# Statistics in one block, fitted planning costs, and an accumulating DMA inside the cross product

## The chip, the cores and the metric

The kernel runs on one core of one Trainium2 chip. Times are device microseconds of one execution; the time of a kernel is the median of its runs. A profile comes from one execution, whose own time is given beside its span. The engines are called as the profile calls them: PE (matrix multiplications, with its weight loads as PEld), DVE (vector), ACT (scalar and activation), POOL (GpSimd) and SP, which here only issues DMAs.

## The reference: what is computed

With q = x, k, v of 2048 x 640 (sequence by channel):

```python
g = sigmoid((x * gate_w).sum(-1, keepdims=True))
# a: causal 4-tap shift of k, times v, then a long convolution along the sequence, times q
kv = k_shift * v
y  = irfft(rfft(pad(kv)) * rfft(pad(ssm_k)))[:S] + kv * ssm_D
a  = q * y
# b: an MLP over the sequence axis
h  = layernorm(x)                       # over the 640 channels
u  = gelu(einsum("bsd,sf->bdf", h, w1) + b1)      # f = 1536
b  = transpose(einsum("bdf,fs->bds", u, w2) + b2)
out = g * a + (1 - g) * b
```

All inputs and the output are bf16.

## The kernel before

The long convolution is done in the frequency domain by matrix products with sine and cosine tables (`FTB`, and its transposed copy `GTB`, written by four DMA transposes). The sequence index is split as 4 residues (p = 0 to 3) by 128 partitions by 4 blocks (hk = 0 to 3); the two halves of the sequence (h = 0, 1) are transformed separately. `fwd` multiplies tables with one half of the weights (`wT`, name W) or of kv (name A); ACT evicts each result from PSUM into one of the arrays `C[0]` to `C[3]`; `mixing` combines the four residues by sums and differences on DVE. W gives the spectra V0 and V1, kv gives A0 and A1. `v1mix` adds one part of the weights' spectra onto another with accumulating DMAs on POOL's queue.

The products of spectra run on DVE in bf16. A spectrum holds slabs of 2560 columns: 1280 columns of one component and 1280 of the other. `cross(g)` (g = 0, 1; i = 0, 1 in each) multiplies A0 by V1 and leaves the result in V1; `y1(g)` forms A1 times V0 in A1 with `product` and adds V1 to it by `acc_dma`, an accumulating DMA on POOL's queue. `product(A0[g], ...)` gives the spectrum of the first half of the output. `invmix` turns spectra into four slabs `Z`, `inverse(h, Z)` multiplies by `GTB`, ACT evicts with the gate as scale into `cgb`, DVE multiplies by q (`q_hi`, `q_lo`) and adds onto the MLP's part in `O1`, and SP writes the rows out. `tm[0]` and `tm[1]` are the DVE's two scratch arrays for products.

Beside it stands the MLP. `ln_tile` takes statistics of one of 16 tiles of X on DVE, `ln_apply` computes the factors on POOL (a power) and normalizes X in place on DVE. Twelve groups of 32 matmuls (name m1, X by the columns of w1 in `ring`) are evicted with Gelu into `GT`; 16 groups of 24 (name m2, `GT` by w2 in `W2`, which takes over the space of `ring`) are evicted by ACT into `O1`. The gate's sums come from DVE products into three buffers `gq` and ACT copies with an accumulator (`gsum`), between the m1 groups.

PSUM has four slots, at most three for the convolution and two for the MLP. **The order on each engine is not that of the program text.** `SC.add` records every operation with a duration estimated by a formula (`dve_dur`, `act_dur`, `mms`, literal numbers for a few), its reads and writes and a priority: the place in the text, or a given number; the lower goes first, and the MLP's matmuls have the highest numbers. `SC.run` then plays a list schedule of all engines from these estimates: each engine takes the ready operation of lowest number. `SC.emit` writes the instructions in that order, with semaphore waits where an operation depends on another engine or a DMA. On the chip every engine executes its list in order, and a late operand holds up all that stands behind it in the list. An element-wise operation of n columns on POOL is charged n/500 + 0.3 us, a DMA of n bytes n/320000 us one after the other and 2.0 us more to its end.

Most helpers issue through a common line: L617 is any `tensor_tensor`, L627 and L628 any `tensor_scalar`, L655 any ACT operation, L293 any matmul, L262 an accumulating DMA, L260 a DMA transpose, L267 any other DMA.

Buffers overlap in place: before, `gq` and `junk` (the output of the gate's ACT copies) lie over `KF`, the taps' array of the k shift; `q_hi` lies over `C[0]`; `q_lo` over the second half of `C[1]`; one of the two arrays `kp`, through which k is transposed, lies over `GTB`.

Of the kernel before, what the change touches and what calls it, by code (L numbers as in the profile page):

```python
# [322 lines left out]
class _Sched:  # L323
# [58 lines left out]
    def run(self):  # L382
# [29 lines left out]
        while started < n:  # L412
# [6 lines left out]
            for e in engs:  # L419
                while pend[e] and pend[e][0][0] <= t:  # L420
                    _, p, i = heapq.heappop(pend[e])
                    heapq.heappush(ready[e], (p, i))
                if free[e] > t:
                    nxt.append(free[e])
                    continue
                skipped = []
                pick = None
                while ready[e]:
                    p, i = heapq.heappop(ready[e])
                    op = ops[i]  # L430
                    if op.vt is not None and op.vt.slot is None:
                        c = op.vt.cls
                        if not nfree or held.get(c, 0) >= self.limit.get(c, 99):
                            skipped.append((p, i))
                            continue
                    pick = op
                    break
                for s in skipped:
                    heapq.heappush(ready[e], s)
                if pick is None:  # L440
                    if pend[e]:
                        nxt.append(pend[e][0][0])
                    continue
                op = pick
                progress = True
                started += 1
                if op.vt is not None and op.vt.slot is None:
                    nfree.sort()
                    op.vt.slot = nfree.pop(0)
                    held[op.vt.cls] = held.get(op.vt.cls, 0) + 1  # L450
                op.start = t
                if e in ("SP", "QA") or op.lat < 0:
                    issue = 0.1
                    s = max(t + issue, dma_free)
                    dma_free = s + op.dur
                    op.end = dma_free + 2.0
                    free[e] = t + issue
                else:
                    op.end = t + op.dur
                    free[e] = op.end  # L460
                order.append(op)
                if op.vt is not None:
                    op.vt.left -= 1
                    if op.vt.left == 0:
                        heapq.heappush(frees, (op.end + 0.05, op.vt.slot, op.vt.cls))
                for s in op.asucc:
# [12 lines left out]
                nxt.append(free[e])  # L479
# [25 lines left out]
def _build(nc, A_q, A_k, A_v, A_shift_k, A_ssm_k, A_ssm_D, B_x, B_w1, B_b1, B_w2, B_b2, gate_w, out):  # L505
# [10 lines left out]
    with ExitStack() as es:  # L516
# [33 lines left out]

        gwb = alloc("gwb", [128, D], BF16)
        Drow = alloc("Drow", [1, D], BF16)
        ident = alloc("ident", [128, 128], BF16)
        KF = alloc("KF", [128, NG, 7, 32], BF16)
# [5 lines left out]
        rstd = alloc("rstd", [128, 16], F32)  # L560
        vtmp = alloc("vtmp", [128, 16], F32)
        gpre = alloc("gpre", [128, 16], F32)
# [157 lines left out]
        def k_turn(hk):  # L720
            o, i = kp[hk % 2], kn[hk % 2]
            ov = o[:, :, :].rearrange("p g (q c) -> p g q c", q=4)
            iv = V(i, 0, [[32, NG], [D, 4], [1, 32]])
            SC.add("DVE", 0.85, lambda s: T.op("DVE", lambda e: e.tensor_copy(ov, iv), [i[:, :, :]], [o[:, :, :]]), [i[:, :, :]], [o[:, :, :]], prio=0, name="kperm")  # L724
            c0 = 16 + 128 * (hk % 2)
# [114 lines left out]
        def ln_tile(hk, p):  # L840
            t = 4 * hk + p
            xs = X[:, hk, p, :]
            for ci in range(2):
                o, i = stats[:, t, 6 * ci:6 * ci + 6], xs[:, 320 * ci:320 * ci + 320]
                SC.add("DVE", 0.46, (lambda o, i: lambda s: T.op("DVE", lambda e: e.bn_stats(o, i), [i], [o]))(o, i), [i], [o])  # L845
            o, i = mv[:, t, :], stats[:, t, :]
            SC.add("DVE", 0.2, (lambda o, i: lambda s: T.op("DVE", lambda e: e.bn_aggr(o, i), [i], [o]))(o, i), [i], [o])
# [84 lines left out]
        for ft in range(FT):  # L932
# [14 lines left out]
            if ft == 0:  # L947
                act(junk[:, :], gwb[:, :], ACT.Copy, acc=gws[:, :], name="gws").after.add(g_)
# [17 lines left out]

        def w2_load(hk):
            for a in range(2):
                dma(W2[hk % 2][:, 6 * a:6 * a + 6, :], dr(B_w2, a * 6 * 128 * S + 512 * hk, [[S, 128], [128 * S, 6], [1, 512]]), 128 * 6144)

        for p in range(4):
            dma(GTB[:, p, :, :, :, :].rearrange("q a b c d -> q (a b c) d"), FTB[:, p, :, :, :, :].rearrange("q a b c d -> q (a b c) d"), 128 * 2048, rate=200.0, transpose=True, prio=10 ** 5)

        HORD = (2, 3, 0, 1)
        for n_, hk in enumerate(HORD):
            w2_load_at = n_
            W2h = W2[n_ % 2]
            for a in range(2):
                dma(W2h[:, 6 * a:6 * a + 6, :], dr(B_w2, a * 6 * 128 * S + 512 * hk, [[S, 128], [128 * S, 6], [1, 512]]), 128 * 6144)
            for p in range(4):  # L980
# [172 lines left out]
```

## Time and profile before

| | |
|---|---|
| median of 3 runs | 198.19 us (197.91 to 199.74) |
| profiled execution | 197.93 us, its span 196.1 us |
| PE busy | 177.4 us (90%) |
| DVE busy | 177.0 us (90%) |
| ACT busy | 118.5 us (60%) |
| POOL busy | 28.6 us (15%) |
| granted PE clock | 0.996 of full |
| HBM read, written | 25.87 MB, 2.62 MB |

A line of the timeline reads: start, length, engine, program line, operation, output<-input by the program's names without buffer numbers, shapes, count, and in brackets the idle time of that engine just before and who released it. Consecutive instructions of one kind are merged into one line with a count. "Issue to landing" of a DMA is the time from its issue to its completion.

### The profile page before, as it was taken

What the parts mean: (1) busy time and instruction counts of PE and PEld (TensorE: products, weight loads), DVE (VectorE), ACT (ScalarE), POOL (GpSimd) and SP (SyncE); (2) the same over time, 40 slices, a digit from 0 to 9 for tenths busy, and PEclk for the clock granted to TensorE, in tenths of its full rate; (3) what the DMA queues carried; (4) which work ended last, traced back from release to release, by engine and by line L of the source; (5) the groups of instructions that cost most, each with busy time, mean ns of one, the idle gap of its engine ahead of it and who ended that gap; (6) DMA issues with size and microseconds to landing.
All of it is one profiled execution on the core that took longest, in us unless ns stands there. A gap on an engine that the chain in (4) does not pass through costs nothing.

```text
span 196.1 us, 3370 instructions
## 1 busy us (share of the span) xinstructions
PE 177.4 (90%) x1403; PEld 131.4 (67%) x1403; DVE 177.0 (90%) x196; ACT 118.5 (60%) x187; POOL 28.6 (15%) x30
## 2 busy tenths in 40 slices
PE   0759987999999999999999999999999979997890
PEld 0546564468767787777777778888888867775560
DVE  7996998799999179999999879999999599989994
ACT  4798967997749793799796413131313117664471
POOL 2629802500005400000000000040400000000000
PEclk9999999999999999999999999999999999999998
DMA  5999999994999999960053008029999960222034
GB/s 162 331 409 379 364 209 253 310 417 143 165 276 265 227 199 191 258 202 0 3 185 135 3 24 282 15 64 232 234 305 231 383 269 5 91 76 101 3 107 160
DMA packets 36719, 37.62 MB, mean 192 GB/s; under 512 B 15579, under 2 KB 32608, under 8 KB 36704
## 3 DMA queue, kind: packets, MB, share of 16 engines
q1 hardware_dynamic: 34464, 32.15, 54.4%
q0 software_dynamic: 2176, 5.24, 14.4%
q8 instruction: 11, 0.18, 0.4%
q14 instruction: 4, 0.03, 0.0%
q10 hardware_dynamic: 64, 0.01, 0.0%
HBM read 25.87 MB, written 2.62 MB: 145 GB/s over the span
## 4 chain that ended last, share of the span: by engine, by line
PE 67%; DVE 16%; DMA 9%; ACT 3%; POOL 2%; issue 2%; SPq 0%; DVEq 0%
PE pp L293 67%; DMA kn<-in_A_k_dram 5%; DMA X<-in_A_q_dram 4%; DVE kp L724 3%; DVE stats L845 2%; DVE C L617 2%; DVE SS L617 2%; DVE X L628 2%; ACT ksh L655 2%; DVE vkv L617 1%; DVE cgb L617 1%; DVE O L617 1%; POOL rstd L617 1%; POOL vtmp L627 1%; ACT cgb L655 1%
## 5 line engine op out<-in xcount | busy, mean ns | idle before, releaser
L293 PE MATMUL pp<-X,ring 128*128 128x320 bf16 x384 | 55.5, 299 | 1.6 <-DVE X L628 1.6
L617 DVE TENSOR_TENSOR C<-C 128x2560 bf16<-128x2560 bf16 (+1 forms) x28 | 48.9, 1773 | 8.3 <-ACT C L655 5.5
L293 PE MATMUL pp<-GT,W 128*128 128x320 bf16 x384 | 52.8, 299 | 1.1 <-ACT O L655 1.1
L293 PEld LDWEIGHTS pp<-GT,W 128*128 128x128 bf16 x384 | 43.5, 113 | 10.0 <-issue 1.4
L293 PEld LDWEIGHTS pp<-X,ring 128*128 128x128 bf16 x384 | 36.6, 98 | 17.6 <-DVE X L628 2.0
L655 ACT ACTIVATE C<-pp 128x640 bf16<-128x640 f32 x64 | 39.9, 723 | 5.5 <-PE pp L293 5.2
L655 ACT ACTIVATE O<-pp,c,omg 128x640 bf16<-128x640 f32 (+1 forms) x17 | 14.5, 853 | 37.9 <-PE pp L293 37.9
L617 DVE TENSOR_TENSOR tm<-C,C 128x2560 bf16<-128x2560 bf16 (+1 forms) x12 | 22.8, 1930 | 0.0
L262 POOL DMA_DIRECT2D C<-C x6 | 7.5, 1406 | 90.1 <-DVE C L617 90.1
L293 PE MATMUL pp<-wT,FTB 128*128 128x320 bf16 x128 | 20.2, 314 | 0.4 <-ACT wT L655 0.4
L655 ACT ACTIVATE GT<-pp,cc 128x640 bf16<-128x640 f32 x12 | 9.5, 792 | 14.6 <-PE pp L293 14.5
L617 DVE TENSOR_TENSOR C<-tm 128x1280 bf16<-128x1280 bf16 (+1 forms) x16 | 18.0, 1154 | 0.1
L293 PEld LDWEIGHTS pp<-wT,FTB 128*128 128x128 bf16 x128 | 11.9, 102 | 7.8 <-ACT C L655 2.3
L655 ACT ACTIVATE cgb<-pp,gg 128x640 bf16<-128x640 f32 x16 | 12.6, 794 | 6.4 <-PE pp L293 3.3
L293 PE MATMUL pp<-C,GTB 128*128 128x320 bf16 x96 | 13.7, 299 | 2.2 <-DVE C L617 2.2
L293 PE MATMUL pp<-ident,ssm 128*128 128x128 bf16 x80 | 8.4, 265 | 6.2 <-DVE pint L617 5.3
L845 DVE BATCH_NORM_STATS2 stats<-X 128x6 f32<-128x320 bf16 x32 | 13.5, 460 | 0.4 <-DMA X<-in_A_q_dram 0.4
L293 PEld LDWEIGHTS pp<-C,GTB 128*128 128x128 bf16 x96 | 9.2, 98 | 6.4 <-DVE C L617 2.5
L655 ACT ACTIVATE junk<-gq 128x640 bf16<-128x640 bf16 x16 | 11.8, 737 | 0.5
L293 PEld LDWEIGHTS pp<-ident,ssm 128*128 128x128 bf16 x80 | 6.5, 127 | 8.0 <-DMA ssm<-in_A_ssm_k_dram 5.3
L655 ACT ACTIVATE wT<-pp 128x640 bf16<-128x640 f32 x16 | 10.2, 711 | 2.6 <-PE pp L293 2.6
L655 ACT ACTIVATE ksh<-pp 128x1024 bf16<-128x1024 f32 (+1 forms) x12 | 9.6, 893 | 3.2 <-PE pp L293 3.2
(63 smaller groups left out, 176.6 us busy)
## 6 DMA issues: line engine op xcount, KB each, us to landing
ring<-in_B_w_dram SPq DMA_DIRECT2D x12, 512.0 KB, 10.9
W<-in_B_w_dram SPq DMA_DIRECT2D x8, 768.0 KB, 6.9
C<-C POOLq DMA_DIRECT2D x6, 640.0 KB, 11.3
ssm<-in_A_ssm_k_dram SPq DMA_DIRECT2D x4, 640.0 KB, 9.0
X<-in_A_q_dram SPq DMA_DIRECT2D x4, 640.0 KB, 9.3
kn<-in_A_k_dram SPq DMA_DIRECT2D x4, 640.0 KB, 8.5
out_dram<-O SPq DMA_DIRECT2D x7, 320.0 KB, 2.3
vkv<-in_A_v_dram SPq DMA_DIRECT2D x2, 640.0 KB, 4.7
```

Source lines behind the costliest of these rows:

```text
L262: ins = engobj.dma_start(out_ap, in_ap, accum_op=ALU.add, max_dma_last_dim=2560)
L293: ins = self.nc.tensor.matmul(ps_ap, lhsT=lhsT, rhs=rhs, start=start, stop=stop, skip_group_check=True)
L617: return SC.add(eng, d, lambda s: T.op(eng, lambda e: e.tensor_tensor(o, a, b, op), [a, b], [o]), [a, b], [o], prio=prio, name="tt")
L627: return e.tensor_scalar(o, a, s1, None, op0=op0)
L628: return e.tensor_scalar(o, a, s1, s2, op0=op0, op1=op1)
L655: return T.op("ACT", lambda e: e.activation(o, src, func, **kw), rr + [src], ww)
L724: SC.add("DVE", 0.85, lambda s: T.op("DVE", lambda e: e.tensor_copy(ov, iv), [i[:, :, :]], [o[:, :, :]]), [i[:, :, :]], [o[:, :, :]], prio ...
L845: SC.add("DVE", 0.46, (lambda o, i: lambda s: T.op("DVE", lambda e: e.bn_stats(o, i), [i], [o]))(o, i), [i], [o])
```

## The change

Six things are changed together:

- **Planning costs.** The constants of `dve_dur`, `act_dur`, `mms`, `kperm`, `bn_stats` and `bn_aggr` are different, and DMAs on POOL's queue are charged 3 us more to their end. These numbers enter no instruction; they enter the order.
- **Statistics.** `ln_apply` is called once after all 16 tiles, on 16 columns, in place of four calls on 4 columns; one more POOL product keeps sqrt(var) in `sd`, which replaces one small DVE product of the gate.
- **Cross product.** The first multiplication of 2560 columns is made into two of 1280 (one into `V1` in place, one into a quarter of `tm[0]`), and their sum is formed by a DMA that accumulates `tm[0]`'s quarter onto `V1`. The other sum stays on DVE, with the two halves of `tm[1]` used in turn.
- **Space of q_hi and gq.** `q_hi` moves over `Drow` and `KF`, and is loaded ahead of the W2 loads in the text; `gq` moves from `KF` over `GTB`; `junk` goes, the ACT copies write in place.
- **q_lo** is loaded only after the last W2 load has been issued.
- **product(A0[0])** stands behind `inverse(1, Z1)` in the text instead of ahead of its `invmix`.

```diff
@@ SC.run
-                    op.end = dma_free + 2.0
+                    op.end = dma_free + 2.0 + (3.0 if e == "POOL" else 0.0)
@@ buffers
+        ident = alloc("ident", [128, 128], BF16)
         Drow = alloc("Drow", [1, D], BF16)
-        ident = alloc("ident", [128, 128], BF16)
...
-        gq = [alloc(f"gq{i}", [128, 2, D], BF16, at=base_of(KF) + 2560 * i) for i in range(3)]
-        junk = alloc("junk", [128, D], BF16, at=base_of(KF) + 7680)
+        gq = [alloc(f"gq{i}", [128, 2, D], BF16, at=base_of(GTB) + 2560 * i) for i in range(3)]
...
-        q_hi = alloc("q_hi", [128, 2, 4, D], BF16, at=base_of(C[0]))
+        q_hi = alloc("q_hi", [128, 2, 4, D], BF16, at=base_of(Drow))
@@ planning costs
-            return n / {1: 960.0, 2: 1920.0, 4: 3840.0}[mode] + (0.1 if mode == 4 else 0.16)
+            return n / {1: 960.0, 2: 1920.0, 4: 3840.0}[mode] + (0.04 if mode == 4 else 0.08)
-            return n / 1200.0 + 0.19 + 0.09 * nap
+            return n / 1200.0 + 0.09 + 0.05 * nap
-            dur = sum(max(n_of(r) / 2400.0, 0.06) for _, _, r, _, _ in items)
+            dur = sum(max(n_of(r) / 2400.0 + 0.0025, 0.056) for _, _, r, _, _ in items)
...
@@ statistics
-        def ln_apply(hk):
-            r = slice(4 * hk, 4 * hk + 4)
-            ts("POOL", vtmp[:, r], mv[:, r, 1], 1e-5, None, ALU.add)
-            tt("POOL", rstd[:, r], vtmp[:, r], V(cst, 1, [[0, 4]]), ALU.pow)
-            for p in range(4):
-                t = 4 * hk + p
-                ts("DVE", X[:, hk, p, :], X[:, hk, p, :], mv[:, t, 0:1], rstd[:, t:t + 1], ALU.subtract, ALU.mult, mode=4, extra=0.17)
+        def ln_apply():
+            ts("POOL", sd[:, :], mv[:, :, 1], 1e-5, None, ALU.add)
+            tt("POOL", rstd[:, :], sd[:, :], V(cst, 1, [[0, 16]]), ALU.pow)
+            tt("POOL", sd[:, :], sd[:, :], rstd[:, :], ALU.mult)
+            for t in range(16):
+                xs = X[:, t // 4, t % 4, :]
+                ts("DVE", xs, xs, mv[:, t, 0:1], rstd[:, t:t + 1], ALU.subtract, ALU.mult, mode=4, extra=0.16)
...
-                    ln_apply(hk)
+                ln_apply()
@@ gate
-                        act(junk[:, :], gb[:, b, :], ACT.Copy, acc=gacc[:, t:t + 1], name="gsum")
-        tt("DVE", gth[:, :], vtmp[:, :], rstd[:, :], ALU.mult, mode=1, prio=0)
-        tt("DVE", gth[:, :], gth[:, :], gacc[:, :], ALU.mult, mode=1, prio=0)
+                        act(gb[:, b, :], gb[:, b, :], ACT.Copy, acc=gacc[:, t:t + 1], name="gsum")
+        tt("DVE", gth[:, :], sd[:, :], gacc[:, :], ALU.mult, mode=1, prio=0)
@@ q_hi (ahead of the W2 loads)
+        for kt in range(2):
+            dma(q_hi[:, kt, :, :], dr(A_q, (1024 + 512 * kt) * D, [[4 * D, 128], [1, 4 * D]]), 128 * 5120)
@@ cross
+        ncr = [0]
         def cross(g):
             for i in range(2):
-                tt("DVE", half(T1, 0), half(A0[g], i), half(V1[g], i), ALU.mult)
-                tt("DVE", half(T1, 1), half(A0[g], i), half(V1[g], i, True), ALU.mult)
-                tt("DVE", comp(V1[g], i, 0), comp(T1, 0, 0), comp(T1, 0, 1), ALU.add)
-                tt("DVE", comp(V1[g], i, 1), comp(T1, 1, 1), comp(T1, 1, 0), ALU.subtract)
+                n_ = ncr[0]
+                ncr[0] += 1
+                tmp = V(tm[0], 1280 * (n_ % 4), [[1, 1280]])
+                tt("DVE", half(T1, n_ % 2), half(A0[g], i), half(V1[g], i, True), ALU.mult)
+                tt("DVE", tmp, comp(A0[g], i, 1), comp(V1[g], i, 1), ALU.mult)
+                tt("DVE", comp(V1[g], i, 0), comp(A0[g], i, 0), comp(V1[g], i, 0), ALU.mult)
+                tt("DVE", comp(V1[g], i, 1), comp(T1, n_ % 2, 1), comp(T1, n_ % 2, 0), ALU.subtract)
+                dma(comp(V1[g], i, 0), tmp, 128 * 5120, stream="POOL", prio=0, accum=True)
@@ the end
-        for kt in range(2):
-            dma(q_hi[:, kt, :, :], dr(A_q, (1024 + 512 * kt) * D, [[4 * D, 128], [1, 4 * D]]), 128 * 5120)
-        product(A0[0], A0[0], V0[0])
         Z1 = invmix(A1[0], A1[1], C3a, None, None)
         inverse(1, Z1)
...
-            dma(q_lo[:, kt, :, :], dr(A_q, 512 * kt * D, [[4 * D, 128], [1, 4 * D]]), 128 * 5120)
+            dma(q_lo[:, kt, :, :], dr(A_q, 512 * kt * D, [[4 * D, 128], [1, 4 * D]]), 128 * 5120).after.add(w2last)
+        product(A0[0], A0[0], V0[0])
         product(A0[1], A0[1], V0[1])
```

More of the change, by code (lines that the diff above doesn't have):

```diff
@@ L560, in _build @@
         rstd = alloc("rstd", [128, 16], F32)
-        vtmp = alloc("vtmp", [128, 16], F32)
+        sd = alloc("sd", [128, 16], F32)
         gpre = alloc("gpre", [128, 16], F32)
@@ L598, in _build @@
         q_lo = alloc("q_lo", [128, 2, 4, D], BF16, at=base_of(C[1]) + 2 * SL * 2)
-        q_hi = alloc("q_hi", [128, 2, 4, D], BF16, at=base_of(C[0]))
+        q_hi = alloc("q_hi", [128, 2, 4, D], BF16, at=base_of(Drow))
+        assert base_of(KF) == base_of(Drow) + 1280
         cgb = [alloc(f"cgb{i}", [128, 2, D], BF16, at=base_of(FTB) + 2560 * i) for i in range(3)]
@@ L723, in k_turn @@
             iv = V(i, 0, [[32, NG], [D, 4], [1, 32]])
-            SC.add("DVE", 0.85, lambda s: T.op("DVE", lambda e: e.tensor_copy(ov, iv), [i[:, :, :]], [o[:, :, :]]), [i[:, :, :]], [o[:, :, :]], prio=0, name="kperm")
+            SC.add("DVE", 0.75, lambda s: T.op("DVE", lambda e: e.tensor_copy(ov, iv), [i[:, :, :]], [o[:, :, :]]), [i[:, :, :]], [o[:, :, :]], prio=0, name="kperm")
             c0 = 16 + 128 * (hk % 2)
@@ L844, in ln_tile @@
                 o, i = stats[:, t, 6 * ci:6 * ci + 6], xs[:, 320 * ci:320 * ci + 320]
-                SC.add("DVE", 0.46, (lambda o, i: lambda s: T.op("DVE", lambda e: e.bn_stats(o, i), [i], [o]))(o, i), [i], [o])
+                SC.add("DVE", 0.38, (lambda o, i: lambda s: T.op("DVE", lambda e: e.bn_stats(o, i), [i], [o]))(o, i), [i], [o])
             o, i = mv[:, t, :], stats[:, t, :]
-            SC.add("DVE", 0.2, (lambda o, i: lambda s: T.op("DVE", lambda e: e.bn_aggr(o, i), [i], [o]))(o, i), [i], [o])
-        def ln_apply(hk):
-            r = slice(4 * hk, 4 * hk + 4)
-            ts("POOL", vtmp[:, r], mv[:, r, 1], 1e-5, None, ALU.add)
-            tt("POOL", rstd[:, r], vtmp[:, r], V(cst, 1, [[0, 4]]), ALU.pow)
-            for p in range(4):
-                t = 4 * hk + p
-                ts("DVE", X[:, hk, p, :], X[:, hk, p, :], mv[:, t, 0:1], rstd[:, t:t + 1], ALU.subtract, ALU.mult, mode=4, extra=0.17)
+            SC.add("DVE", 0.12, (lambda o, i: lambda s: T.op("DVE", lambda e: e.bn_aggr(o, i), [i], [o]))(o, i), [i], [o])
+        def ln_apply():
[5 more added lines that the diff above has]
+                ts("DVE", xs, xs, mv[:, t, 0:1], rstd[:, t:t + 1], ALU.subtract, ALU.mult, mode=4, extra=0.16)
         srcW = lambda h: (lambda kt, p, ci: wT[:, 2 * h + kt, p, 320 * ci:320 * ci + 320])
@@ L947, in _build @@
             if ft == 0:
-                act(junk[:, :], gwb[:, :], ACT.Copy, acc=gws[:, :], name="gws").after.add(g_)
+                act(gq[2][:, 0, :], gwb[:, :], ACT.Copy, acc=gws[:, :], name="gws").after.add(g_)
             if ft in (1, 3, 5, 7):
@@ L965, in _build @@
         tt("DVE", c2[:, :].rearrange("p (a b) -> p a b", a=4), omg[:, :].rearrange("p (a b) -> p a b", a=4), b2f, ALU.mult, mode=1, prio=0)
-        def w2_load(hk):
-            for a in range(2):
-                dma(W2[hk % 2][:, 6 * a:6 * a + 6, :], dr(B_w2, a * 6 * 128 * S + 512 * hk, [[S, 128], [128 * S, 6], [1, 512]]), 128 * 6144)
         for p in range(4):
@@ L974, in _build @@
         HORD = (2, 3, 0, 1)
+        for kt in range(2):
+            dma(q_hi[:, kt, :, :], dr(A_q, (1024 + 512 * kt) * D, [[4 * D, 128], [1, 4 * D]]), 128 * 5120)
         for n_, hk in enumerate(HORD):
-            w2_load_at = n_
             W2h = W2[n_ % 2]
             for a in range(2):
-                dma(W2h[:, 6 * a:6 * a + 6, :], dr(B_w2, a * 6 * 128 * S + 512 * hk, [[S, 128], [128 * S, 6], [1, 512]]), 128 * 6144)
+                w2last = dma(W2h[:, 6 * a:6 * a + 6, :], dr(B_w2, a * 6 * 128 * S + 512 * hk, [[S, 128], [128 * S, 6], [1, 512]]), 128 * 6144)
             for p in range(4):
```

## The prediction

> **What bounds the kernel now.** I read the busy shares and the slices first, then a table of five stretches, then the timeline at the places where the matrix engine stands still.
>
> ```profile
> PE 177.4 (90%) x1403; PEld 131.4 (67%) x1403; DVE 177.0 (90%) x196; ACT 118.5 (60%) x187; POOL 28.6 (15%) x30
> ```
>
> ```profile
> 24.00:40.00 16.00, 13.94 (x117) 8.63 (x115) 14.14 (x37) 13.09 (x23) 3.94 (x5) 1.00 1.13 267
> 56.00:156.00 100.00, 99.92 (x776) 77.13 (x777) 89.98 (x67) 55.04 (x94) 9.93 (x8) 1.00 0.70 175
> 156.00:180.00 24.00, 22.93 (x168) 17.62 (x166) 23.15 (x20) 12.41 (x17) 0.00 (x0) 1.00 0.33 127
> 180.00:192.00 12.00, 9.08 (x65) 5.92 (x64) 11.29 (x11) 6.83 (x9) 0.00 (x0) 1.00 0.16 56
> ```
>
> The columns after the stretch and its length are the busy time of PE, weight load, DVE, ACT and POOL, then clock, DMA share and GB/s. PE and DVE look equally loaded over the whole span, but between 56 and 156 us PE is busy for 99.92 of 100. The MLP products fill every hole there, so in that stretch no saving on DVE, ACT or a DMA shortens anything by itself. What can be won is PE's idle time outside it: 2.06 us between 24 and 40, 1.07 between 156 and 180, 2.92 between 180 and 192 (0.7 of that is after the last matmul), and the tail. The two late holes:
>
> ```profile
> 154.25 1.49 DVE L617 TENSOR_TENSOR C<-C 128x2560 bf16<-128x2560 bf16 x1 [2.57 <-DMA C<-C]
> 158.11 4.51 PE L293 MATMUL pp<-GT,W 128*128 128x320 bf16 x32 [1.07 <-ACT O L655]
> 180.09 0.62 ACT L655 ACTIVATE O<-pp,c,omg 128x320 bf16<-128x320 f32 x1 [1.01 <-PE pp L293]
> 182.28 4.63 PE L293 MATMUL pp<-C,GTB 128*128 128x320 bf16 x32 [2.22 <-DVE C L617]
> 142.99 1.41 SPq L267 DMA_DIRECT2D W<-in_B_w_dram  x2
> 144.44 6.64 SPq L267 DMA_DIRECT2D q_lo<-in_A_q_dram  x1
> 151.13 3.37 SPq L267 DMA_DIRECT2D q_hi<-in_A_q_dram  x2
> 130.00:160.00 30.00, 28.93 (x214) 23.94 (x212) 27.40 (x15) 7.96 (x9) 4.63 (x4) 1.00 1.02 277
> ```
>
> At 158.11 the first matmuls of the last W2 block start. ACT is named, but its eviction is an ordinary one; the block's weights were issued at 142.99 into DMA engines with a share of 1.02 over 130 to 160, together with q_lo, q_hi and two pairs of accumulating DMAs. I read the 1.07 us as W2 landing late. The last W2 half is evicted at 180.09, released by PE; from 180.05 on PE has nothing left but the last inverse, and waits 2.22 us for DVE. So the end is set by DVE's chain through the cross products and y1, and before that by a crowded DMA.
>
> **The change, part by part.**
>
> *Cross products.* Each of the four steps had two multiplications of 2560 columns and two sums of 1280; now one of 2560 and three operations of 1280.
>
> ```profile
> 86.14 2.89 DVE L617 TENSOR_TENSOR tm<-C,C 128x2560 bf16<-128x2560 bf16 x2
> 89.67 1.56 DVE L617 TENSOR_TENSOR C<-tm 128x1280 bf16<-128x1280 bf16 x2
> 123.71 2.83 DVE L617 TENSOR_TENSOR tm<-C,C 128x5120 bf16<-128x5120 bf16 x1
> 111.67 0.17 DVE L617 TENSOR_TENSOR gth<-gth,gacc 128x16 f32<-128x16 f32 x1 [0.56 <-ACT junk L655]
> 114.54 0.17 DVE L628 TENSOR_SCALAR gg<-gth 128x16 f32<-128x16 f32 x1 [1.14 <-ACT gth L655]
> C<-C POOLq DMA_DIRECT2D x6, 640.0 KB, 11.3
> DMA to landing us min/median/max: 7.7/11.7/15.3
> 88.00:128.00 40.00, 40.00 (x297) 30.01 (x295) 37.93 (x35) 22.31 (x45) 0.00 (x0) 1.00 0.25 80
> ```
>
> A pair of 2560 columns takes 2.89, a single one 1.49 (the row at 154.25), so one behind another costs 1.40; two of 1280 take 1.56, 0.78 each. Each step saves 0.62 us, four save **2.5 us of DVE**. Against that stand four accumulating DMAs of 320 KB on POOL. Their engine is free (0.00 busy between 88 and 128) and the DMA share there is 0.25. But all four read `tm[0]`, and y1's first product writes the whole of `tm[0]`: it must wait until the last of them has landed. y1's other product (2.83 us into `tm[1]`) can go first. The landing of 320 KB is not in the trace. The 640 KB ones took 7.7 to 15.3; half the bytes in a quiet stretch I put at half the median, 5.6, with 0 and 15.3 as ends. So DVE waits 5.6 - 2.8 = 2.8 us (0 to 12.5), and behind it queue everything of y1, the product of A0 and the inverse mixing. The Trainium skill, "DMA: Bandwidth & Descriptors", section "Latency and other measured facts", gives a fixed cost of about 2 us for a DMA and about 1 us to the first byte from this queue; an estimate from that page would be some 3 us beside the transfer itself, and the wait would be under 2 us. No run here shows it yet.
>
> *Waits of DVE that go.* Before, DVE stood 0.56 and 1.14 us on the gate and 2.57 us on the accumulating DMA ahead of the inverse mixing. The mixing of the second half now has precedence over the product of A0[0] (8.4 us), which fills the time of that DMA, and the queue is emptier. I count these 4.3 us as gone (0 to 4.3). Together: 2.5 + 4.3 - 2.8 = 4.0 us earlier for Z0, at 178.3 instead of 182.28. The W2 products would end at 180.05 - 1.07 = 179.0. So the hole of **2.2 us** closes, with 0.7 us to spare; if none of the waits went it would widen by 0.3.
>
> *q_hi, q_lo.* q_hi moves to the space of Drow and KF, which is dead when the last kv group is done, and q_lo is held behind the last W2 load. That takes 1.3 of some 8 MB out of 130 to 160 and lets W2 pass. **1.07 us** goes (0 to 1.07). The last four ring loads may get q_hi beside them; the MLP reads those weights after eight of its twelve column blocks, well inside the stretch where PE never waited, so nothing is charged (1.3 MB at 277 GB/s would be 4.7 us if it did).
>
> *The tail.*
>
> ```profile
> 191.34 0.79 ACT L655 ACTIVATE cgb<-pp,gg 128x640 bf16<-128x640 f32 x1 [0.23 <-PE pp L293]
> 192.17 0.83 DVE L617 TENSOR_TENSOR cgb<-cgb,q_lo 128x1280 bf16<-128x1280 bf16 x1 [0.49 <-ACT cgb L655]
> 193.03 0.96 DVE L617 TENSOR_TENSOR O<-cgb,O 128x640 bf16<-128x640 bf16 x3
> ```
>
> Now the last matmul belongs to the inverse, followed by 0.79 + 0.83 + 0.96 us. If Z0 comes early, the inverse goes first (its priority is the lower number) and a W2 half closes: 0.62 and one sum of 320 columns, about 0.3. That is **1.6 us** less; 0 if the inverse stays last. With so little to spare I take half, 0.8.
>
> *Statistics in one block.*
>
> ```profile
> 10.02 0.19 DVE L847 BATCH_NORM_AGGREGATE mv<-stats 128x2 f32<-128x12 f32 x1
> 10.88 0.19 DVE L847 BATCH_NORM_AGGREGATE mv<-stats 128x2 f32<-128x12 f32 x1
> 19.04 1.16 DVE L628 TENSOR_SCALAR X<-X,mv,rstd 128x640 bf16<-128x640 bf16 x3 [1.61 <-POOL rstd L617]
> 20.33 4.35 DVE L724 COPY kp<-kn 128x2560 bf16<-128x2560 bf16 x1
> 19.97 4.03 POOL L617 TENSOR_TENSOR KF<-cw,m 128x2240 bf16<-128x2240 bf16 x1
> 25.31 0.81 DVE L724 COPY kp<-kn 128x2560 bf16<-128x2560 bf16 x1
> 29.51 0.23 POOL L627 TENSOR_SCALAR vtmp<-mv 128x4 f32<-128x4 f32 x1 [5.51 <-DVE mv L847]
> 29.82 1.04 POOL L617 TENSOR_TENSOR rstd<-vtmp,cst 128x4 f32<-128x4 f32 x1
> 38.78 1.51 DVE L628 TENSOR_SCALAR X<-X,mv,rstd 128x640 bf16<-128x640 bf16 x4
> PE pp L293 <- DVE X L628: 1.6, 3, 0.8
> 28.30 3.68 ACT L655 ACTIVATE wT<-pp 128x640 bf16<-128x640 f32 x6 [0.29 <-PE pp L293]
> ```
>
> Before, four blocks of four tiles each went through POOL (0.23 and 1.04 us), and X was normalized from 19.04 to 40.3. Now all sixteen tiles come first: the first is aggregated at 10.02, the others 0.86 apart, so the last ends near 23.1; one copy of kn (0.8) falls among them, then POOL takes 0.23 and a power over 16 columns. That power is not in the trace: from 1.04 (cost by instruction) to 4.2 (by column). Taking the 0.23 row as the fixed part leaves 0.2 us per column, so 3.4. Then 16 tiles at 0.36. X starts near 27.5 and is whole at 33.3, seven microseconds earlier than before at the end, but eight later at the start. PE meanwhile has the second half's transposes and forward products, paced by ACT at 0.61 us an eviction. POOL's two KF operations no longer have the powers between them, so the second ends at about 21.6 and the copy at 20.33, which took 4.35 us beside it against 0.81 alone, stands at most 1.3. The Trainium skill, "SBUF — State Buffer", section "Who interferes with whom", says a copy on DVE and an operation on GpSimd take one pair of ports as an exclusive lock; by that rule the copy gets back the whole of its stall when KF is over. The 4.35 against 0.81 agrees.
>
> The order written out before the run charges this power 16/500 + 0.3 = 0.33 us; PE executes in order, so X being 3.1 us later than planned can stop PE behind its first X product. That costs 0 to 3.1, and the present 2.06 us of idle time can go: the bounds are -2.1 and +3.1. I take **+1.0**, because the 1.6 us that PE stood for X before came from the same undercharged power, 1.04 against 0.31, and there is now one such place instead of four.
>
> *gq into GTB.*
>
> ```profile
> 19.91 6.50 SPq L260 DMA_TRANSPOSE GTB<-FTB  x1
> 56.41 10.31 SPq L260 DMA_TRANSPOSE GTB<-FTB  x3
> 111.45 0.19 ACT L655 ACTIVATION_READ_ACCUMULATOR junk<-gq 128x1 f32 x1
> W<-in_B_w_dram SPq DMA_DIRECT2D x8, 768.0 KB, 6.9
> 117.62 12.47 PEld L293 LDWEIGHTS pp<-GT,W 128*128 128x128 bf16 x92
> ```
>
> The four transposes into GTB must now follow the last gate sum, at about 111.6 instead of 19.9 and 56.4. They hold SP's queue for 3.4 us each while they issue, to about 125.4. The second W2 block, free to load at 117.6, is behind them; W2 took 6.9 us to land, so it is there at 132.3, and its products are due 13 us after 117.7, at 130.7: up to 1.6 us of PE. With a quiet DMA the transposes issue faster. The charge is 0 to 1.6 (12 if each took the 6.50 of the first). I take 0.5. The fitted constants save no time themselves; their order can put PE behind something late. For the other slips in order I add 0.5, half of the hole at 158.11 (0 to 3).
>
> **Sum**, against the profiled execution of 197.93 (196.1 of span and 1.8 around it): -2.2 - 1.07 - 0.8 + 1.0 + 0.5 + 0.5 = -2.1, so 195.8. The median of the three runs is 198.19, 0.3 above; I forecast **196.0**.
>
> **Rivals.**
> 1. *All of it comes through.* Idle time at 24 to 40 goes, W2 closes the kernel, nothing new waits: -2.2 - 1.07 - 1.6 - 2.06 = -6.9, 191.3. For it: fewer POOL round trips, an emptier DMA late. Against it: the power over 16 columns.
> 2. *The early part eats it.* PE stands 3.1 us behind X, the late holes close: +0.1, 198.2. For it: POOL's 1.04 for four columns. Against it: PE has 24 groups of other work there, if the order puts them first.
> 3. *`tm[0]` is the new wait (slower).* If the last cross DMA lands over 9.6 us after the last cross product, DVE loses more than the 6.8 it gains and Z0 is later than now. At the row's 15.3 the loss is 12.5 - 6.8 = 5.7 at the end: 203.6, or some 201 with the other gains. For it: the whole of DVE's work after y1 queues there. Against it: DMA share 0.25, half the bytes.
> 4. *The change doesn't do what it says.* The new order hides no wait, holes move: 198.
>
> **How the numbers follow.** Forecast 0.48, rival 1 0.17, rival 2 0.12, rival 4 0.10, rival 3 with the held-up W2 0.13. A measurement of this kernel tells about 1% (2 us) from no change. Faster than 196.2: rival 1 and most of the forecast's case, whose own range is 193.5 to 197.5: 0.17 + 0.41 = 0.58. Slower than 200.2: 0.13. Same: 0.29. The range runs from rival 1's 191.3 to 199.2, past rivals 2 and 4.
>
> **What would show it.** The table of stretches: PE's idle time at 24 to 40 (2.06 now), and the two late holes; the four accumulating DMAs near 90 to 125 and what DVE's first write of `tm` after them waits for; POOL's power over 128x16; the transposes into GTB and the W2 load behind them. A PE hole over 3 us before 40 or ahead of an inverse would make the forecast wrong.

## The result, and the profile after

The changed kernel takes 192.72 us (median of 4 executions, 192.67 to 192.85). The kernel before, run beside it, took 198.91 (4 executions, 197.91 to 199.74). The ratio is 0.969, interval 0.964 to 0.975: 3.1% faster, where 1.1% (196.0 us) was forecast. The profiled execution has a span of 190.9 us against 196.1, so 5.2 us are to be found in the two traces. The kernel before has executions near 198.0 and near 199.6, and its medians say mostly how many of them fell into each.

The table of stretches of the kernel after (length, busy time of PE, weight load, DVE, ACT, POOL, then clock, DMA share, GB/s), and under it one row of before:

```profile
24.00:40.00 16.00, 14.93 (x120) 9.42 (x118) 12.78 (x23) 14.27 (x25) 7.44 (x4) 1.00 1.11 274
40.00:56.00 16.00, 14.94 (x159) 11.28 (x158) 15.86 (x13) 13.17 (x21) 0.00 (x0) 1.00 0.73 198
56.00:150.00 94.00, 93.98 (x742) 71.53 (x740) 90.90 (x68) 48.35 (x85) 13.39 (x12) 1.00 0.84 210
150.00:180.00 30.00, 30.00 (x221) 22.25 (x220) 24.54 (x23) 17.21 (x23) 0.00 (x0) 1.00 0.25 91
```

```profile
40.00:56.00 16.00, 15.78 (x175) 12.22 (x174) 15.86 (x13) 11.65 (x16) 0.00 (x0) 1.00 0.87 226
```

PE is busy for 177.4 us in both traces, so all of the 5.2 us is time in which PE stands still. From 56 us on it does not stand still any more. Both late holes (1.07 and 2.22 us) are gone: 3.3 us. Between 24 and 40 its idle time fell from 2.06 to 1.07. Between 40 and 56 it rose from 0.22 to 1.06: one matmul there waits 1.04 us for DVE. The early part as a whole is within 0.2 us of before. The end, in the timeline:

```profile
171.29 4.54 PE L293 MATMUL pp<-C,GTB 128*128 128x320 bf16 x32
180.02 7.77 PE L293 MATMUL pp<-GT,W 128*128 128x320 bf16 x56
187.83 0.62 ACT L655 ACTIVATE O<-pp,c,omg 128x320 bf16<-128x320 f32 x1 [1.01 <-PE pp L293]
188.48 0.33 DVE L617 TENSOR_TENSOR O<-cgb,O 128x320 bf16<-128x320 bf16 x1 [1.30 <-ACT O L655]
```

The last inverse starts at 171.29, not 182.28, and 56 matmuls of W2 (7.77 us) are left behind it. The kernel ends with a W2 half, 0.62 and 0.33 us behind PE: from the last matmul to the end of the span it is 3.1 us, where it was 4.8. So 3.3 (holes) + 1.7 (tail) + 0.2 (early part) make up the 5.2.

Why Z0 comes 11 us earlier is seen where the forward products of the second half end, PE's line of after and then two of before:

```profile
77.02 3.42 PE L293 MATMUL pp<-kv,FTB 128*128 128x320 bf16 x24
81.37 1.79 PE L293 MATMUL pp<-kv,FTB 128*128 128x320 bf16 x12
```

```profile
87.33 1.79 PE L293 MATMUL pp<-kv,FTB 128*128 128x320 bf16 x12
90.05 1.79 PE L293 MATMUL pp<-kv,FTB 128*128 128x320 bf16 x12
```

Before, 3 or 4 groups of four matmuls stood between two MLP blocks of 8; after, 6 or 7. The last one ends at 83.2 instead of 91.8, and DVE's work behind it starts 8 us earlier. Nothing in the operations asks for that: it is PE's list that is different. ACT, which evicts each group, was not the limit that the old charges made of it. Its evictions of 640 columns between those blocks, of before and then of after, start about 0.60 us apart in both, and before it even stood 0.68 us waiting for PE:

```profile
82.10 2.49 ACT L655 ACTIVATE C<-pp 128x640 bf16<-128x640 f32 x4 [0.68 <-PE pp L293]
77.77 3.68 ACT L655 ACTIVATE C<-pp 128x640 bf16<-128x640 f32 x6
```

The rows of after that answer to the other steps:

```profile
C<-tm POOLq DMA_DIRECT2D x4, 320.0 KB, 6.1
111.95 2.82 DVE L617 TENSOR_TENSOR tm<-C,C 128x5120 bf16<-128x5120 bf16 x1 [1.90 <-DMA C<-tm]
87.75 9.11 SPq L260 DMA_TRANSPOSE GTB<-FTB  x4
27.07 2.94 POOL L617 TENSOR_TENSOR rstd<-sd,cst 128x16 f32<-128x16 f32 x1
51.75 3.75 PE L293 MATMUL pp<-vkv,FTB 128*128 128x320 bf16 x26 [1.04 <-DVE vkv L617]
```

### The profile page after: what moved, and what is told of

Its sections match the earlier page's. It is cut to its first block, busy times and chain, and to the rows that moved or that the text cites. A ratio compares the mean times of both kernels' runs of the same rounds, so it can differ in the third digit from the quotient of the medians.

```text
span 190.9 us, 3358 instructions
## 1 busy us (share of the span) xinstructions
PE 177.4 (93%) x1403; PEld 130.5 (68%) x1403; DVE 170.3 (89%) x195; ACT 116.4 (61%) x187; POOL 33.0 (17%) x29
## 4 chain that ended last, share of the span: by engine, by line
PE 71%; DVE 19%; DMA 4%; POOL 2%; issue 2%; SPq 0%; ACT 0%; DVEq 0%
PE pp L293 71%; DVE stats L845 6%; DMA X<-in_A_q_dram 4%; DVE X L628 3%; DVE SS L617 3%; DVE C L617 2%; DVE kp L724 2%; POOL rstd L617 2%; DVE vkv L617 1%; DVE mv L847 1%; POOL sd L627 1%; SPq L267 0%; ACT O L655 0%; DVE O L617 0%; DVEq L187 0%
## 5 line engine op out<-in xcount | busy, mean ns | idle before, releaser
L293 PE MATMUL pp<-X,ring 128*128 128x320 bf16 x384 | 54.0, 299 | 0.1
L293 PEld LDWEIGHTS pp<-X,ring 128*128 128x128 bf16 x384 | 37.1, 98 | 15.4 <-DVE X L628 0.7
L617 DVE TENSOR_TENSOR tm<-C,C 128x2560 bf16<-128x2560 bf16 (+2 forms) x12 | 20.2, 1708 | 1.9 <-DMA C<-tm 1.9
L293 PE MATMUL pp<-wT,FTB 128*128 128x320 bf16 x128 | 19.6, 310 | 0.6 <-ACT wT L655 0.4
L617 DVE TENSOR_TENSOR C<-tm 128x2560 bf16<-128x2560 bf16 (+1 forms) x12 | 15.0, 1263 | 0.1
L655 ACT ACTIVATE gq<-gq 128x640 bf16<-128x640 bf16 x16 | 11.8, 756 | 0.0
L617 DVE TENSOR_TENSOR tm<-C,SS 128x5120 bf16<-128x5120 bf16 x4 | 11.2, 2817 | 0.0
```

The lines of the kernel that those rows point to most:

```text
L293: ins = self.nc.tensor.matmul(ps_ap, lhsT=lhsT, rhs=rhs, start=start, stop=stop, skip_group_check=True)
L617: return SC.add(eng, d, lambda s: T.op(eng, lambda e: e.tensor_tensor(o, a, b, op), [a, b], [o]), [a, b], [o], prio=prio, name="tt")
L655: return T.op("ACT", lambda e: e.activation(o, src, func, **kw), rr + [src], ww)
```

## The experiments

All are built from the kernel before or the changed one. Times are medians; the kernel before, run beside each group, took 198.04 and 198.12 us (runs 1 to 8) and 199.57 (runs 9 to 12). The changed kernel was not run again beside the groups. The executions of before near 198.0 spread over 0.3 us, so differences of 0.2 to 0.4 us between versions are at the edge of what these runs resolve. Every edit goes through the planner: each version has an order of its own on every engine, and what a run shows is the worth of an edit together with the new order that it brings. In the diffs the changed parts go by the names of the list of changes.

**1. Planning costs alone.**

```diff
 the kernel before
+ planning costs (SC.run, dve_dur, act_dur, mms, kperm, bn_stats, bn_aggr)
```

> The kernel before with only the planning costs of the change (SC.run, dve_dur, act_dur, mms, kperm, bn_stats, bn_aggr). Theory 1, the order decides: the new costs let PE put seven forward groups in a row instead of three or four, so the last forward products are evicted some 8 us earlier, DVE's chain to Z0 has slack, the hole of 2.22 us ahead of the last inverse closes and a W2 half ends the kernel (1.6 us less of tail); the 1.07 us at the last W2 block may stay: 3 to 5 us faster than before. Theory 2, the operations decide (cross product, product order, loads), and the constants only shuffle: within 1 us of before.

193.38 us (193.35 to 193.51), 0.976 of before (0.972 to 0.980): 4.7 us, with not one operation different. PE has no hole from 56 us to the last matmul, and W2 products are last. What it lacks against the changed kernel stands between 40 and 56 us (13.36 against 14.94 busy); between 24 and 40 it is ahead (15.66 against 14.93):

```profile
40.00:56.00 16.00, 13.36 (x147) 10.06 (x145) 15.82 (x12) 10.36 (x14) 0.00 (x0) 1.00 0.45 157
182.85 5.60 PE L293 MATMUL pp<-GT,W 128*128 128x320 bf16 x40
```

The 1.07 us at the last W2 block, which I had expected might stay, is gone, though all the loads stand where they were in the text. So crowded DMA engines were not shown to be its cause, and the traces speak for another. In before and in run 5, which has the same wait, it ends 0.14 us behind an eviction by ACT. The eviction ahead of the W2 block in before, and PE's row in run 5:

```profile
157.08 0.89 ACT L655 ACTIVATE O<-pp,c,omg 128x640 bf16<-128x640 f32 x1 [2.38 <-PE pp L293]
155.85 3.42 PE L293 MATMUL pp<-GT,W 128*128 128x320 bf16 x24 [1.07 <-ACT O L655]
```

The eviction of before ends at 157.97, and PE goes on at 158.11; in run 5 the same eviction ends at 155.71, and PE goes on at 155.85. The wait is the 0.89 of that eviction and 0.18 around it in both. The last W2 load was issued at 144.0 in before and at 142.1 in run 5, and no W2 load took longer than 13.5 and 13.0 us to land, so all had landed by 157.5 and 155.1, ahead of the eviction's end. Most likely the plan gave these matmuls the PSUM slot that was just being evicted; which slot it was is not in the trace.

**2. All but the planning costs.**

```diff
 the changed kernel
- planning costs
```

> The changed kernel with the planning costs of before. Theory 1: DVE's chain gains only the 4.0 us that were counted before the run; Z0 comes at about 178, the hole closes with nothing to spare, the tail stays as it was: 2 to 3.5 us faster than before, 2 to 4 slower than the changed kernel. Theory 2: equal to the changed kernel within 0.5 us.

198.73 us (197.17 to 199.76), 1.002 of before (0.999 to 1.005): nothing is left. I had expected 2 to 3.5 us. Z0 is late by 1.34 us, and PE runs into the normalization of X early, with more behind it than the wait itself:

```profile
34.12 2.29 PE L293 MATMUL pp<-X,ring 128*128 128x320 bf16 x8 [2.67 <-DVE X L628]
34.00:35.00 1.00, 0.89 (x4) 0.52 (x5) 1.00 (x3) 0.00 (x0) 0.23 (x1) 0.50 0.83 297
183.13 4.54 PE L293 MATMUL pp<-C,GTB 128*128 128x320 bf16 x32 [1.34 <-DVE C L617]
```

In the second row the clock granted to PE, third from the end, is 0.50 of full, and eight matmuls take 2.29 us where eight take 1.25 elsewhere.

**3. All but the cross product.**

```diff
 the changed kernel
- cross() with one sum by an accumulating DMA
+ cross() of before
```

> The changed kernel with the cross product of before (four DVE operations, no accumulating DMA in it). Theory 1: Z0 has over 5 us of slack, DVE's 2.5 us and the wait of 1.9 us on the DMA are both off the path: within 0.5 us of the changed kernel. Theory 2: 2.5 us of DVE come back at the end: 1.5 to 2.5 us slower than the changed kernel.

192.88 us (192.84 to 193.0), 0.2 from the changed kernel, as theory 1 has it. The inverse even starts earlier than with the DMA (171.29):

```profile
169.21 4.58 PE L293 MATMUL pp<-C,GTB 128*128 128x320 bf16 x32
```

That is not because the DMA costs the chain more than it spares. Up to the mixing for the first inverse (Z1) DVE is 2.6 us earlier with the DMA, the wait of 1.90 us on `tm[0]` included. Behind it, with the DMA, DVE waits three times, 1.27, 1.35 and 0.76 us, for evictions of the first inverse, where run 3 waits once for 0.23. Two rows of the changed kernel, then two of run 3:

```profile
143.98 4.29 DVE L617 TENSOR_TENSOR C<-C 128x2560 bf16<-128x2560 bf16 x3
155.91 0.83 DVE L617 TENSOR_TENSOR cgb<-cgb,q_hi 128x1280 bf16<-128x1280 bf16 x1 [1.35 <-ACT cgb L655]
146.54 4.29 DVE L617 TENSOR_TENSOR C<-C 128x2560 bf16<-128x2560 bf16 x3
156.00 0.83 DVE L617 TENSOR_TENSOR cgb<-cgb,q_hi 128x1280 bf16<-128x1280 bf16 x1 [0.23 <-ACT cgb L655]
```

So the 2.5 us of DVE are saved, and the order of the lists spends them again before the last inverse. Neither shows in the time, because PE is full.

**4. All but the places and loads.**

```diff
 the changed kernel
- gq over GTB, q_hi over Drow and KF, its early load, q_lo behind the last W2 load, product(A0[0]) behind inverse(1)
+ all of these as before
```

> The changed kernel with the places of gq, junk, q_hi, the loads of q_hi and q_lo, and the position of the product of A0[0] as before. Theory 1: the DMA engines are crowded again at 130 to 160 us and the hole at the last W2 block comes back, 0.5 to 1.1 us slower than the changed kernel, while the slack of Z0 hides the later inverse mixing. Theory 2: the order of the products and loads is what the gain is: 3 us or more slower than the changed kernel.

192.32 us (192.2 to 192.47): 0.4 faster than the changed kernel, where 0.5 to 1.1 slower was expected. No hole comes back at W2, and between 40 and 56 PE is fuller (14.94 in the changed kernel):

```profile
40.00:56.00 16.00, 15.67 (x165) 11.75 (x164) 15.83 (x12) 13.08 (x20) 0.00 (x0) 1.00 0.66 191
```

**5. One constant: ACT's charge.**

```diff
 the kernel before
-            return n / 1200.0 + 0.19 + 0.09 * nap
+            return n / 1200.0 + 0.09 + 0.05 * nap
```

> The kernel before with one formula changed: ACT operations are charged n/1200 + 0.09 + 0.05 per operand instead of n/1200 + 0.19 + 0.09. PE's list then has 5 to 6 forward groups between two MLP blocks (24, 20, 20 matmuls of A0) instead of 2 to 4. Theory 1 (the forward products come earlier, and with them all of DVE's chain): the last of them are evicted 5 us or more earlier, Z0 is no longer late, the hole of 2.2 us goes: 2.5 to 4.5 us faster than before; the inverse stays last in PE's list, so the tail stays. Theory 2 (DVE's charges decide, because they place the inverse in PE's list): within 1 us of before.

193.72 us (193.2 to 194.0), 0.975 of before (0.969 to 0.980). One formula that enters no instruction gives 4.4 us. The eviction of 640 columns was charged 0.72 us and is now charged 0.62; a forward group of four matmuls is charged 0.53. In the traces consecutive evictions stand 0.60 apart. With the old charge the plan thinks PE must wait for ACT after 3 or 4 groups and puts an MLP block there; with the new one it finds the next PSUM slot free in time for longer, and the trace has 5 or 6 groups. The rows show the early part full, the last inverse with no wait ahead of it, and the W2 hole still there (28.93 of 30):

```profile
24.00:40.00 16.00, 15.53 (x132) 10.44 (x131) 14.35 (x35) 14.91 (x26) 6.36 (x8) 1.00 1.11 275
40.00:56.00 16.00, 15.97 (x167) 11.97 (x167) 15.13 (x12) 14.43 (x21) 0.00 (x0) 1.00 0.85 243
150.00:180.00 30.00, 28.93 (x212) 22.15 (x209) 27.68 (x25) 14.53 (x20) 0.00 (x0) 1.00 0.36 132
177.87 4.62 PE L293 MATMUL pp<-C,GTB 128*128 128x320 bf16 x32
```

The 4.4 is not the 4.7 of run 1 over again. Here 1.8 us come from the stretch between 24 and 56 us (0.50 idle, 2.28 before) and 2.2 from the hole ahead of the last inverse, while the W2 hole and the long tail (4.8) stay. In run 1 it is the two late holes and the tail, and the early part is 0.7 worse than before.

**6. The other charges.**

```diff
 the kernel before
+ planning costs, but act_dur as before
```

> The kernel before with all changed planning costs but the one of ACT. PE's list has 2 to 4 forward groups between MLP blocks as before, but 12 matmuls of m2 behind the last inverse. Theory 1: DVE's chain starts as late as before, and PE, now told to have the inverse earlier, waits for Z0: within 1.5 us of before. Theory 2: 3 us or more faster.

197.47 us (197.32 to 199.0), 0.996 of before (0.993 to 1.000): as theory 1 has it in size, but not in cause. PE does not wait for Z0: the last inverse starts at 181.78 with no wait ahead of it. There is one wait of 0.88 us ahead of the first inverse (Z1), and the larger ones are early, for X:

```profile
29.20 1.43 PE L293 MATMUL pp<-X,ring 128*128 128x320 bf16 x8 [2.15 <-DVE X L628]
37.64 1.85 PE L293 MATMUL pp<-X,ring 128*128 128x320 bf16 x8 [2.39 <-DVE X L628]
```

**7. All but the block of statistics.**

```diff
 the changed kernel
- ln_apply() once on 16 columns
+ ln_apply(hk) four times on 4 columns, as before
```

> The changed kernel with the statistics in four blocks of four tiles as before. Theory 1: the block is worth little, since the early part of PE gained 0.2 us in all; the four powers of 1.04 us between the KF operations hold up the copy of kn again: 0.3 to 1.5 us slower than the changed kernel. Theory 2 (the block is the gain): 3 us or more slower.

195.40 us (194.51 to 196.43), 0.984 of before (0.977 to 0.991). 1.8 to 3.7 us slower than the changed kernel: more than theory 1 had, less than theory 2 at the lower end. X is not where PE waits (15.66 of 16 busy between 24 and 40). In the profiled execution (196.43, mean clock 0.991) it waits at the first forward products of kv, and then runs at half clock:

```profile
55.37 4.84 PE L293 MATMUL pp<-vkv,FTB 128*128 128x320 bf16 x22 [1.62 <-DVE vkv L617]
56.00:58.00 2.00, 2.00 (x9) 1.15 (x8) 2.00 (x1) 1.41 (x3) 0.00 (x0) 0.50 1.02 195
```

The two shorter executions (194.5) have a mean clock of 1.000, so 1.8 us of the loss stand without the half clock and about as much more goes with it. So the block is worth something, and through DVE's later work, not through X itself. It has less effect under the old order (run 2), where other waits lie in front.

**8. Planning costs and the block.**

```diff
 the kernel before
+ planning costs
+ ln_apply() once on 16 columns, with its product in the gate
```

> The kernel before with the planning costs and the one block of statistics alone: old cross product, old places and loads. Theory 1: these two are all of the gain, the rest gives nothing or costs (without the places 192.3 was measured, without the cross product 192.9, with all 192.7): 192 to 192.9. Theory 2 (the cross product and the places carry part of the gain when the other is missing): 193.7 or more.

194.05 us (193.35 to 194.25), 0.976 of before (0.971 to 0.981): a miss. It is not better than the costs alone, 1.7 us behind run 4, from which it differs by the cross product only. The profiled execution (193.35) has no hole between 40 and 56 us but one ahead of the first inverse, for which the profile names no releaser:

```profile
150.82 4.56 PE L293 MATMUL pp<-C,GTB 128*128 128x320 bf16 x32 [0.89 <-issue]
```

So the cross product, worth 0.2 us when the loads are moved (run 3), is worth 1.0 (profiled executions) to 1.7 us (medians) when they are not. Its slower executions take 0.9 us more at a mean clock of 0.999 to 1.000, so it is not the clock; none was profiled, and the cause stays open.

**9. All but ACT's charge.**

```diff
 the changed kernel
-            return n / 1200.0 + 0.09 + 0.05 * nap
+            return n / 1200.0 + 0.19 + 0.09 * nap
```

> The changed kernel with the planning charge of ACT alone as before (n/1200 + 0.19 + 0.09 per operand). PE's list has 2 to 3 forward groups between two MLP blocks again. Theory 1 (the charge of ACT carries the gain, through the length of these runs): the last forward products end 5 us or more later than in the changed kernel, Z0 later still, PE waits again: 196 to 198.5. Theory 2 (any of the other parts closes the holes as well): within 1 us of the changed kernel's 192.7.

197.77 us (196.64 to 198.09), 0.992 of before (0.988 to 0.995). The size is as expected, the place is not. Z0 is in time here: the inverse starts at 179.88 with no wait. The loss is early, at one wait of 4.04 us for X and some 6 us at half clock behind it:

```profile
30.77 2.29 PE L293 MATMUL pp<-X,ring 128*128 128x320 bf16 x8 [4.04 <-DVE X L628]
32.00:34.00 2.00, 2.00 (x15) 1.58 (x14) 2.00 (x7) 0.37 (x1) 0.00 (x0) 0.50 0.80 151
```

So ACT's charge works in two places. With it too high, PE's list also puts MLP products ahead of the transposes of the second half, and PE gets to them before X is there.

**10 and 11. More work on DVE.**

```diff
 the changed kernel
         product(A0[0], A0[0], V0[0])
+        for _ in range(2):        # 4 in the second
+            tt("DVE", P2(T0), P2(A0[0]), P2(A0[0]), ALU.mult)
         product(A0[1], A0[1], V0[1])
```

> The changed kernel with two more DVE products of 5120 columns (2 x 2.75 = 5.5 us, into scratch that nothing reads) between the product of A0[0] and that of A0[1]. Theory 1: PE starts the last inverse at 171.3 and has 7.8 us of W2 products left behind it, so Z0 may come 7.8 us later at no cost: within 0.4 us of the changed kernel. Theory 3 (DVE's time still sets the end, one for one): 4 to 5.5 us slower than the changed kernel.

> The same with four more such products, 11 us. Theory 1: this is past the 7.8 us: Z0 comes 3.2 us after the last W2 product and the inverse is last again with its longer tail (1.6 us): 4 to 6 us slower than the changed kernel, 196.7 to 198.7. Theory 3: 10 to 11 us slower.

With 5.5 us more: 193.04 us (192.98 to 193.12), 0.3 more than the changed kernel. With 11 us more: 198.71 (197.03 to 198.92), 6.0 more; its shorter executions, at 197.1, lie in the expected range (196.7 to 198.7), the others at its upper end or up to 0.2 above. The inverse in the first, and in the second with the clock behind it:

```profile
177.46 4.54 PE L293 MATMUL pp<-C,GTB 128*128 128x320 bf16 x32
```

```profile
181.53 6.18 PE L293 MATMUL pp<-C,GTB 128*128 128x320 bf16 x32 [2.30 <-DVE C L617]
183.00:184.00 1.00, 1.00 (x6) 0.56 (x4) 1.00 (x1) 0.62 (x1) 0.00 (x0) 0.50 0.00 0
```

DVE's chain has slack of more than 5.5 and less than 11 us, which agrees with the 7.8 us of W2 products behind the inverse. The added work also changes the plan: in the first of the two the list itself puts the inverse later, with 12 matmuls of W2 behind it. Theory 3, DVE one for one, falls.

**12. Two blocks.**

```diff
 the kernel of run 4
-                ln_apply()
+                    if hk % 2:
+                        ln_apply(hk // 2)      # 8 columns; add and power charged 0.8 and 1.7 us
```

> The version that was fastest so far (costs, one block, cross product, without the moved places and loads: 192.3), with the statistics in two blocks of eight tiles and POOL's add and power charged 0.8 and 1.7 us instead of 0.31 each. In that version PE idled 1.0 us between 24 and 30 us, behind ACT's evictions of the second half's weights, because X was not ready. Theory 1: X of the first two blocks is ready some 5 us earlier, an MLP block fills part of that: 191.5 to 192.3. Theory 2 (the powers get between the two KF operations and hold up the copies of kn, as with four blocks): 192.5 to 195.

190.73 us (190.6 to 191.21), 0.959 of before (0.954 to 0.964): the fastest version, 2.0 us ahead of the changed kernel and 1.6 of run 4, and better than either theory had. MLP products stand among the transposes at 28.39, 2.2 us before X was begun in the changed kernel's order (30.05 on DVE, 30.64 on PE), and the early part is nearly full:

```profile
28.39 1.25 PE L293 MATMUL pp<-X,ring 128*128 128x320 bf16 x8
24.00:40.00 16.00, 15.28 (x128) 10.49 (x128) 14.40 (x25) 14.56 (x25) 5.47 (x5) 1.00 1.10 277
40.00:56.00 16.00, 15.97 (x169) 12.11 (x167) 15.83 (x11) 14.45 (x21) 1.41 (x2) 1.00 0.78 214
54.16 2.96 PE L293 MATMUL pp<-vkv,FTB 128*128 128x320 bf16 x20
21.73 2.26 POOL L852 TENSOR_TENSOR rstd<-sd,cst 128x8 f32<-128x8 f32 x1
```

All of the 1.6 us is won before 56 us: the 20 forward matmuls at 54.16 start at 55.78 in run 4, with as many MLP matmuls ahead of them. In the two stretches PE is busy 0.56 us longer than in run 4; the rest lies in time in which PE counts as busy in both, and why is not shown. Which of the two edits (blocks, charges) brings it was not taken apart.

## Why the prediction was right or wrong

The reading of what bounds the kernel held: PE from 56 us on, the two late holes and the tail; the cause given for the first of the holes did not. The direction held too, and that the time lies in the range is luck, as the step on which the gain rests was charged as a loss. The size was wrong, 2.2 us forecast against 6.2 in the medians and 5.2 in the profiled executions.

- **The step that failed is the one on the fitted constants:** "The fitted constants save no time themselves; their order can put PE behind something late", with 0.5 us charged for slips. I counted them on the wrong side. Alone they gave 4.7 us (run 1), ACT's formula alone 4.4 (run 5), and without them the rest gave nothing (run 2). In the changed kernel they lengthen the runs of forward groups in PE's list from 3 or 4 to 6 or 7, DVE's chain starts 8 us earlier, and the hole of 2.2 and 1.7 of the tail go. I had the numbers: the charge is in the code, and ACT's evictions stand 0.6 us apart in the timeline. What I left out is to ask what an overcharged engine does to the list of the engine that feeds it.
- **Z0, forecast at 178.3 with 0.7 us to spare,** came at 171.3 with 7.8 to spare. The terms were about right (DVE waited 1.90 us for the DMA on `tm[0]`, forecast 2.8; the landing took 6.1, forecast 5.6; the waits on the gate went), but the start of the chain moved by 8 us, which the sum had not. As PE was full, the surplus was worth nothing beyond the 2.2 us of the hole and the shorter tail: in run 10 most of it is used up, for 0.3 us. A slip in the prediction: rival 2's +0.1 comes out at -0.2 by its own terms (3.1 - 2.2 - 1.07).
- **The tail** was charged half, 0.8, because so little was to spare. With Z0 early it was the whole of it, 1.7 measured.
- **The statistics:** the power over 16 columns took 2.94 us (forecast 3.4), X starts at 30.05 (forecast 27.5), because the last tile is aggregated at about 25.4, not 23.1, and POOL's add ahead of the power took 1.39, not 0.23. The charge of +1.0 for PE standing behind X did not fall due, because the list puts the transposes and two forward groups first. In runs 2, 6 and 9, with other lists, PE did stand behind X: 2.7, 4.5 (run 6, with the four blocks of before) and 4.0 us.
- **The W2 hole** went (1.07), but my reading of it as W2 landing late was wrong. Runs 1 and 4 keep the loads where they were and have no such hole, and in before and run 5 the wait ends with an eviction by ACT, after W2 had landed (run 1). So it came from the order, and that the forecast for it came true is luck.
- **GTB behind the gate's sums:** forecast to hold SP from 111.6 to 125.4. The sums were done by 94 and the four transposes issued from 87.75 to 96.9 in quiet DMA engines, 2.3 us each. No charge, where 0.5 was taken. (The 12 us given there for four transposes of 6.50 would by its own terms be about 14.)
- **The cross product,** which the title names, is worth 0.2 us in this kernel (run 3) and 1.0 to 1.7 without the moved loads (run 8 against run 4); the moved places and loads cost 0.4 (run 4).

Three terms account for the profiled difference from my sum of 2.1: the tail (0.8 forecast, 1.7 measured: 0.9), the early part (+1.0 forecast, -0.2 measured: 1.2), and the two allowances of 0.5 that were not used (1.0): 3.1 together, 5.2 less 2.1. The remaining microsecond between 5.2 and 6.2 lies in the executions of before that took 199.6: the profiled one was at 197.93.

## What to carry to other kernels

Where a program orders its own instructions from estimated durations, an estimate is part of the kernel: read the spacing of each engine's commonest operation from the trace and compare it with its charge, above all for the engine that sits between two others. Once PE is full in the profile, ask of every saving elsewhere which hole of PE it closes, and stop counting when the holes are closed. Charge slow odd operations (a power on POOL) at what they take; with that and a finer split of the statistics, not taken apart, run 12 is 1.6 us ahead of run 4 and 2.0 of the changed kernel.

## What the hardware showed that was not expected

A hole on PE of 2 to 4 us can cost more than its length, because the granted clock falls to 0.50 behind it, or from within it on. It stayed there for about 3.4 us in runs 2, 6, 7 and 11 and about twice as long in run 9. It was seen at waits of 1.62 (run 7, with short ones ahead of it), 2.30 (run 11), 2.39 (run 6), 2.67 (run 2) and 4.04 us (run 9). It was not seen behind the 2.15 of run 6 and the 2.22 of the profiled execution of before, so the length of the hole alone does not decide. In run 11, 32 matmuls behind such a hole took 6.18 us against 4.54, so 1.6 us were lost beside the 2.3. Two groups of executions about 1.6 us apart go with it in run 11, 197.1 at a mean clock of 0.995 and 198.7 at 0.989, and in run 7, 194.5 at 1.000 and 196.3 at 0.991. The kernel before has two such groups (198.0 at 0.998, 199.6 at 0.988) and a hole of 2.22 us at the same place; that its longer executions are those where the clock falls there is an inference, as none of them was profiled. Run 6 is a warning: it has executions at 197.4 and at 199.0 with the same mean clock of 0.991, so the mean clock alone does not tell the groups apart, and where the half clock falls must matter too. The Trainium skill, "TensorE: Matmul & The Clock Gate", section "Part 1: The HAM clock gate (the "warmup" mystery)", says that the clock halves after an idle window of about 3.4 us, and that the window runs freely. The halving agrees, and so does the length if it is taken for the time at half clock; the holes here that set it off are shorter, from 2.3 us on in runs 2, 6 and 11, and by the measurement a gap under 3.4 us is not safe.
